# Seven load buffers instead of ten, and the casts of later head pairs tied to the scores three pairs back

## The chip, the cores and the metric

The kernel runs on one core of a Trainium2 chip. The metric is the device time of one execution in microseconds, as the median over executions. The profile is one execution taken by the hardware profiler; its span is a little shorter than the device time. Names in the profile: PE is TensorE's matmuls, PEld its weight loads, DVE is VectorE, ACT ScalarE, POOL GpSimd, SP SyncE; SPq and POOLq are their DMA queues. L491 is line 491 of the kernel; lines differ by a few between versions. An execution counts as slow when it takes over 1.5% longer than the fastest of the same kernel, and as fast otherwise; only fast ones are compared. The granted clock is the share of its full speed that TensorE was given.

## The reference, cut to what matters

```python
# attention: batch 4, 8 heads, 768 tokens, head size 64
scores = q @ k.T / 8;  masked by blocks of 32;  attn = softmax(scores);  x = attn @ v
# then a mixing block on x (4, 768, 512)
u  = x + lam * (w_tok @ (alpha1 * x + beta1))
out = u + lam * (relu((alpha2 * u + beta2) @ w_ch1) @ w_ch2)
```

The kernel handles the heads in 16 pairs, numbered 0 to 15, and runs attention of later pairs beside the mixing of earlier batches.

## The kernel before

The kernel is written as a list of jobs with priorities. A list scheduler in the kernel's own code decides, at build time, in which order each engine's instructions stand; on the chip each engine runs its own list strictly in that order and waits with semaphores. So a change of one dependency can move many instructions, and an instruction that waits holds up everything behind it on its engine.

From pair 6 on, q and k reach TensorE in four steps: a load by GpSimd's queue into a buffer "ld"; a cast by VectorE into a staging tile "rel"; two DMA transposes by SyncE's queue into qx and kx; the score matmuls. V takes only a load and a cast.

```python
slots = dict(sps=2, mm=2, cp=1, ops=1, eT=NET, head=NQB, vext=NV, ld=10, rel=2, ...)

ld[p, nm] = load(nm, pair_ap(src, *pairs[p]), [P, 2, NT * D], dt, "ld", 10, ...)   # 192 KB each

# pairs 6 to 15
rels[p] = wk.tile([P, 2, NT, P], BF, name="rel", tag="rel", bufs=2)
cq = cast_job(p, 0, "q2", stage_of(p, 0), (3, p, 0), ("rel",))        # VectorE
ck = cast_job(p, 1, "k2", stage_of(p, 1), (3, p, 1), (), [cq])        # VectorE
def xt(p=p):                                                          # SyncE
    for i, dst in enumerate((qx, kx)):
        nc.sync.dma_start_transpose(dst[slot_of(p)]..., rels[p][:, i, :, :]...)
# ... cut: scores, exp on ScalarE, mask minimum on VectorE, attn @ v, mixing
```

An eviction, below, is the instruction that takes a finished matmul result out of TensorE's result buffer; the ReLU eviction writes the tile "hts". A mask minimum (tile "eT") applies the mask to a piece of the attention weights.

There are two staging tiles. The q cast of pair p writes the tile that pair p-2 used, so it waits until both transposes of pair p-2 have landed.

The softmax here doesn't subtract the row's maximum and nothing guards it: scores larger than these inputs give would overflow.

Of the kernel before, what the change touches and what calls it, by code (L numbers as in the profile page):

```python
# [21 lines left out]
D = 64  # L22
# [5 lines left out]
P = 128  # L28
NT = S // P
# [6 lines left out]
NU = 9  # L36
NS = NPAIR * NU
NPE = 6
NET = 11
LEAD = 18  # L40
AHEAD = 13000.0
SCALE = 1.0 / 8.0
EXPB = -0.35667494
# [21 lines left out]
def kernel(  # L65
# [47 lines left out]
    NQB = 4  # L113
    NV = 3
# [6 lines left out]
    vext = [  # L121
        pp.tile([P, 2, NT, VW], F16, name=f"vext{i}", tag=f"vext{i}") for i in range(NV)
    ]
# [18 lines left out]
    def pair_ap(src, b, n):  # L142
        return src[b, 2 * n : 2 * n + 2].rearrange("h (p o) d -> p h (o d)", o=NT)
# [54 lines left out]
    def first_cast(a):  # L198
        for i, src in enumerate((q2f, k2f)):
            sl = src[:, a, :].rearrange("p (o d) -> p o d", o=NT)  # L200
            dst = rel0[:, a, :, i * D : (i + 1) * D]
            if a == 0 and i == 1:
                nc.scalar.copy(out=dst, in_=sl)
            else:
                nc.vector.tensor_copy(out=dst, in_=sl)
# [25 lines left out]
    for j in range(2, NQB):  # L231
# [11 lines left out]
    DRAIN = 166.0  # L243
    free_at = dict(NONE=0.0, PE=T0, ACT=T0, DVE=T0, POOL=4800.0, SP=T0)
    slots = dict(
        sps=2, mm=2, cp=1, ops=1, eT=NET, head=NQB, vext=NV, ld=10, rel=2,
        x=NXB, uT=3, hts=2, a1p=2, ub=2, ot=2, w2b=1,
    )
    jobs = []
# [35 lines left out]
    def mmt(n, cols):  # L285
        return n * (max(cols, 60) / 2.4 + 2.7)

    def dve(n, rate, base):
        return base + n / 0.96 / rate

    pairs = [(b, n) for b in range(B) for n in range(NPAIR)]
# [4 lines left out]
    def Load(xfer, prio, fn, deps=(), take=()):  # L296
        j = Job("POOL", 720.0, prio, fn, deps, take)
        j.xfer = xfer
        return j

    def load(name, src_ap, shape, dt, tag, bufs, xfer, prio, deps=(), take=()):
        def fn():
            t = wk.tile(shape, dt, name=name, tag=tag, bufs=bufs)
            nc.gpsimd.dma_start(t[:], src_ap)
            return t

        return Load(xfer, prio, fn, deps, take)

    ld = {}
# [4 lines left out]
    def load_pair(p, prio, which="qkv"):  # L314
        for src, dt, nm in ((q, BF, "q2"), (k, BF, "k2"), (v, F16, "v2")):
            if p == 0 and nm != "v2" or nm[0] not in which:
                continue
            ld[p, nm] = load(
                nm, pair_ap(src, *pairs[p]), [P, 2, NT * D], dt, "ld", 10,
                1300.0 if p < 2 else 980.0, prio, take=("ld",),  # L320
            )

# [72 lines left out]
    for t in range(NT):  # L395
# [9 lines left out]
        j = Job("PE", mmt(NT, P), (5, t), tr, [wload["tok", t // 2]], take=("mm",))  # L405
# [25 lines left out]
    for g in range(4):  # L431
# [16 lines left out]
        j = Job("PE", mmt(16, 64), (5, 20 + g), bmm, [j_be2] + [wload["w1", i] for i in range(4)], take=("mm",))  # L448
# [34 lines left out]
    j = Job("DVE", 400.0, (3, 3, 9), mrow, [wtok_jobs[-1]])  # L483
    j = Load(5000.0, mout_prio, mout, [j])
# [4 lines left out]
    def cast_job(p, i, nm, dst_of, prio, take, deps=()):  # L489
        def fn():  # L490
            nc.vector.tensor_copy(  # L491
                out=dst_of(), in_=tl_ld(p, nm).rearrange("p h (o d) -> p h o d", o=NT)
            )

        return Job("DVE", dve(768, 4, 155), prio, fn, [ld[p, nm]] + list(deps), take=take, give=("ld",))

    def tl_ld(p, nm):
        return ld[p, nm].out[:]

    head_ready = {}  # L500

    def slot_of(p):
        return (2 * NPE + p - NPE) % NQB

    rels = {0: rel0}
    for p in range(len(pairs)):
        if p == 0:

            def fc():
                first_cast(1)  # L510

            def f_tr():
                tl["h0"] = transposes(rel0, 1)

            def f_cq(eng):
                copy(eng, qx[1][0:D, :], tl["h0"][0:D, :])

            def f_ck(eng):
                copy(eng, kx[1][0:D, :], tl.pop("h0")[D:P, :])

            head_ready[0] = Job("DVE", 1.0, (0, 0), lambda: None, take=("head", "rel"))
            j = Job("DVE", 720.0, (2, 0), fc)
            j = Job("PE", mmt(NT, P), (2, 0), f_tr, [j], take=("mm",))
            j = Copy((1, 0, 1), f_cq, [j, head_ready[0]], take=("head",))
            j = Copy((1, 0, 2), f_ck, [j], give=("mm", "rel"))

            def f_mb():
                nc.vector.tensor_copy(out=qx[1][MB, :], in_=qx[0][MB, :])

            jb = Job("DVE", 350.0, (2, 0, 1), f_mb)  # L530
            head_ready[1] = Job("NONE", 0.0, (0,), lambda: None, [j, jb], lat=0.0)
        elif p < NPE:

            def rel_of(p, i):
                def f():
                    if i == 0:
                        rels[p] = wk.tile([P, 2, NT, 2 * D], BF, name="rel", tag="rel", bufs=2)
                    return rels[p][:, :, :, i * D : (i + 1) * D]

                return f  # L540

            cq = cast_job(p, 0, "q2", rel_of(p, 0), (2, p, 0), ("rel",))
            ck = cast_job(p, 1, "k2", rel_of(p, 1), (2, p, 1), (), [cq])
            prev = head_ready[2 * p - 1]
            for a in range(2):
                h = 2 * p + a

                def tr(p=p, a=a, h=h):
                    tl["hd", h] = transposes(rels[p], a)

                def cpq(eng, h=h):
                    copy(eng, qx[h % NQB][0:D, :], tl["hd", h][0:D, :])

                def cpk(eng, h=h):
                    copy(eng, kx[h % NQB][0:D, :], tl["hd", h][D:P, :])

                jt = Job("PE", mmt(NT, P), (2, p, a), tr, [ck, prev], take=("mm", "head"),
                         give=("rel",) if a else ())
                j1 = Copy((1, p, a), cpq, [jt])
                j2 = Copy((1, p, a), cpk, [jt])  # L560
                prev = head_ready[h] = Job("NONE", 0.0, (0,), lambda: None, [j1, j2], give=("mm",), lat=0.0)
        else:

            def stage_of(p, i):
                def f():
                    if i == 0:
                        rels[p] = wk.tile([P, 2, NT, P], BF, name="rel", tag="rel", bufs=2)
                    return rels[p][:, i, :, :].rearrange("p o (h d) -> p h o d", h=2)

                return f  # L570

            cq = cast_job(p, 0, "q2", stage_of(p, 0), (3, p, 0), ("rel",))
            ck = cast_job(p, 1, "k2", stage_of(p, 1), (3, p, 1), (), [cq])

            def xt(p=p):
                for i, dst in enumerate((qx, kx)):
                    nc.sync.dma_start_transpose(
                        dst[slot_of(p)][:].rearrange("p (o c) -> p o c", o=NT),
                        rels[p][:, i, :, :].rearrange("p o c -> p (o c)"),
                    )  # L580

            prev = [head_ready[2 * NPE - 1]] if p == NPE else [head_ready[2 * p - 2]]
            jx = Job("SP", 2600.0, (1, p), xt, [ck] + prev, take=("head",), lat=2500.0,
                     give=("rel",))
            jx.slow = True
            head_ready[2 * p] = head_ready[2 * p + 1] = jx
# [4 lines left out]
    qk_jobs, exp_jobs = {}, {}  # L591
    eTs, ops = {}, {}
# [199 lines left out]
    for p in range(len(pairs)):  # L792
        b, n = pairs[p]

        def pv_put(p=p):
            nc.vector.tensor_copy(
                out=vext[p % NV][:, :, :, 0:D],
                in_=tl_ld(p, "v2").rearrange("p h (o d) -> p h o d", o=NT),
            )

        putv[p] = Job("DVE", dve(768, 4, 155), (2 if p == 0 else 3, p, 2), pv_put, [ld[p, "v2"]],
                      take=("vext",), give=("ld",))
        if p >= NPE:
            paired(p)
        else:
            single(p)


    uTs = {}
    ut_jobs = {}  # L810
    for p in range(len(pairs)):
# [67 lines left out]
        if b == 0:  # L879
# [9 lines left out]
            j = Job("PE", mmt(NT, P), (2, p, 9), utr, ubs, take=("mm",), give=("ub",))  # L889
# [16 lines left out]
    for kk in range(2 * B):  # L906
        b, hf = divmod(kk, 2)
        relus = []
        for f in range(16):
# [18 lines left out]
            def rl(eng, kk=kk, f=f):  # L928
# [5 lines left out]
                else:  # L934
# [11 lines left out]
            j = Job("PE", mmt(4, HS), (5, kk, f), c1, deps, take=take,  # L946
                    give=("uT",) if hf == 1 and f == 15 else ())
# [82 lines left out]
    def gated(j):  # L1030
        return j.gate is not None and j.gate >= NS and j.gate - NS > st["ch"] / rate + LEAD

# [20 lines left out]
    while left:  # L1053
        moved = True
        while moved:
            moved = False
            for e in free_at:
                if free_at[e] > t:
                    continue
                best = None  # L1060
                if e == "POOL" and dma_free[0] - t > AHEAD:
                    seq += 1
                    heapq.heappush(events, (dma_free[0] - AHEAD, -seq, None))
                    continue
# [10 lines left out]
                j = best[1]  # L1075
# [45 lines left out]
        while events and events[0][0] <= t:  # L1121
            _, _, j = heapq.heappop(events)
# [45 lines left out]
```

## Time and profile before

| | before |
|---|---|
| median of the first group of runs | 325.51 us (324.99 to 326.92) |
| span of the profiled run | 324.5 us |
| PE busy | 305.8 us, 94% |
| DVE, ACT busy | 206.8, 208.1 us, 64% each |

TensorE is the limit, but not all the time. The windows view gives the busy microseconds of each engine in a stretch (the count of its instructions in brackets). These lines are of the kernel before.

```profile
70.00:80.00 10.00, 9.95 (x135) 7.04 (x133) 8.94 (x21) 7.77 (x9) 5.33 (x8) 1.00 1.46 180
80.00:90.00 10.00, 7.91 (x85) 5.04 (x85) 6.90 (x13) 6.41 (x9) 1.65 (x3) 1.00 1.36 161
90.00:100.00 10.00, 6.29 (x51) 3.12 (x51) 5.37 (x12) 5.29 (x7) 1.39 (x2) 1.00 1.42 139
100.00:110.00 10.00, 9.89 (x108) 5.22 (x109) 9.22 (x19) 5.76 (x8) 2.80 (x4) 1.00 1.04 155
```

The first number after the stretch's length is PE; then come PEld, DVE, ACT, POOL, the granted clock, and two figures of the DMA engines. From 80 to 100 us TensorE is busy 14.20 of 20 us, so it loses 5.80 us there. TensorE's weight loads and VectorE too are less busy in that stretch than on either side of it, so neither is short of time there: something makes them wait. The waits view of the kernel before names it (who waited for whom: us in total, times, longest).

```profile
DVE rel L491 <- DMA kx<-rel: 7.7, 2, 4.6
PE mm L920 <- DVE hts L935: 3.7, 2, 3.5
PE mm L920 <- DVE x_sb L857: 1.9, 1, 1.9
```

VectorE stood twice, 7.7 us together, at a q cast that waited for a kx transpose. TensorE in turn waited for VectorE. VectorE's timeline of the kernel before (start, duration, instruction, in brackets the idle time before it and what ended it) shows what stood behind the two casts.

```profile
87.09 0.36 DVE L491 COPY rel<-q 128x768 bf16<-128x768 bf16 x1 [3.10 <-DMA kx<-rel]
...
92.69 0.36 DVE L491 COPY rel<-k 128x768 bf16<-128x768 bf16 x1
93.01 0.69 DVE L747 TENSOR_TENSOR eT<-eT,maskT 128x1024 f16<-128x1024 f16 x1
98.34 0.36 DVE L491 COPY rel<-q 128x768 bf16<-128x768 bf16 x1 [4.63 <-DMA kx<-rel]
98.61 0.61 DVE L935 TENSOR_SCALAR hts<-mm,b1t 128x384 bf16<-128x384 f32 x1
99.14 0.68 DVE L747 TENSOR_TENSOR eT<-eT,maskT 128x1024 f16<-128x1024 f16 x1
...
107.31 0.35 DVE L796 COPY vext<-v 128x768 f16<-128x768 f16 x1
```

The cast at 87.09 is pair 9's, the one at 98.34 pair 10's. Behind the second stands the ReLU eviction of 98.61, whose input was complete by about 94.5 us. The last line, pair 9's v cast, is a landmark. TensorE waited for that eviction, by its own timeline:

```profile
95.20 0.60 PE L716 MATMUL sps<-qx,kx 64*128 64x512 bf16 x4
99.28 0.81 PE L920 MATMUL mm<-uT,w1b 128*128 128x384 bf16 x4 [3.47 <-DVE hts L935]
```

### The profile page before, as it was taken

The page shows a single profiled execution, that of the slowest core. Times are in us where ns is not written, and L with a number is a line of the kernel's source. Part 1 is how long each engine was busy: PE and PEld are TensorE (multiplying, and loading weights), DVE is VectorE, ACT ScalarE, POOL GpSimd, SP SyncE. Part 2 cuts the span into 40 slices and gives each one's busy share as a digit, 9 for nine tenths or more (in the row PEclk, how much of TensorE's full clock was granted, in tenths as well). Part 3 has the DMA queues.
Part 4 walks back from the last instruction along what each step waited for, and adds up shares of the span by engine and source line. Part 5 has one row for each costly group of instructions (what it writes and reads, how often), then busy time and mean ns, then how long its engine had stood idle before and what let it go on. Part 6 is the DMA issues. An engine that isn't in the chain of part 4 may idle for free.

```text
span 324.5 us, 7574 instructions
## 1 busy us (share of the span) xinstructions
PE 305.8 (94%) x3209; PEld 189.3 (58%) x3238; DVE 206.8 (64%) x406; ACT 208.1 (64%) x264; POOL 44.2 (14%) x69
## 2 busy tenths in 40 slices
PE   7889989899777999999999999999999999999996
PEld 3566868667434556654655655655655565455544
DVE  4559876778657987786969687776878660201001
ACT  4999998897664567866666667755783625354530
POOL 4747312425102201000000000000000000000000
PEclk9999989999999999999999999999999999999999
DMA  5999999999999974304042231003010201201102
GB/s 138 193 247 210 208 242 164 250 189 166 161 123 171 165 138 73 52 34 105 34 43 64 59 85 24 2 34 89 3 26 34 57 34 24 94 5 40 59 19 79
DMA packets 46774, 31.95 MB, mean 98 GB/s; under 512 B 27516, under 2 KB 42264, under 8 KB 46612
## 3 DMA queue, kind: packets, MB, share of 16 engines
q0 software_dynamic: 16496, 17.83, 32.9%
q1 hardware_dynamic: 29992, 13.40, 20.6%
q8 instruction: 25, 0.41, 0.5%
q10 hardware_dynamic: 252, 0.24, 0.3%
q14 instruction: 9, 0.07, 0.1%
HBM read 32.04 MB, written 7.47 MB: 122 GB/s over the span
## 4 chain that ended last, share of the span: by engine, by line
PE 78%; DMA 10%; ACT 7%; DVE 3%; issue 1%; POOL 0%; DVEq 0%; ACTq 0%
PE mm L920 22%; PE cp L965 21%; PE mm L847 8%; PE ops L774 8%; PE sps L716 7%; ACT eT L653 6%; DMA w2b<-in_moe_w_ch_dram 6%; DMA kx<-rel 4%; PE ops L965 4%; PE sps L638 2%; PE sps L920 2%; PE cp L168 1%; ACT kx L268 1%; PE ops L678 1%; DVE hts L935 1%
## 5 line engine op out<-in xcount | busy, mean ns | idle before, releaser
L742 ACT ACTIVATE eT<-sps 128x1024 f16<-128x1024 f32 x90 | 88.3, 1020 | 29.9 <-PE sps L716 28.7
L920 PE MATMUL mm<-uT,w1b 128*128 128x384 bf16 x472 | 90.6, 326 | 5.9 <-DVE hts L935 3.7
L931 ACT ACTIVATE hts<-mm,b1t 128x384 bf16<-128x384 f32 x91 | 52.9, 581 | 62.0 <-PE mm L920 59.4
L965 PE MATMUL cp<-w2b,hts 128*128 128x512 bf16 (+1 forms) x308 | 75.7, 374 | 1.5
L747 DVE TENSOR_TENSOR eT<-eT,maskT 128x1024 f16<-128x1024 f16 x90 | 61.2, 687 | 15.5 <-ACT eT L742 15.4
L920 PEld LDWEIGHTS <-w1b 128*128 128x128 bf16 x512 | 47.1, 97 | 40.2 <-issue 10.1
L653 ACT ACTIVATE eT<-sps 128x1024 f16<-128x1024 f32 (+1 forms) x55 | 52.9, 1016 | 5.8 <-PE sps L638 5.1
L965 PEld LDWEIGHTS <-hts 128*128 128x128 bf16 x400 | 36.4, 98 | 33.6 <-issue 0.8
L982 DVE TENSOR_TENSOR ot<-x_sb,cp 128x512 f32<-128x512 f32 (+1 forms) x21 | 14.1, 673 | 45.9 <-PE cp L965 45.5
L774 PEld LDWEIGHTS <-eT 128*128 128x128 f16 x720 | 29.9, 97 | 16.1 <-issue 3.8
L847 PE MATMUL mm<-a1p,wtokT 128*128 128x128 bf16 x576 | 37.0, 220 | 0.1
L638 PE MATMUL sps<-qx,kx 88*128 88x512 bf16 (+1 forms) x144 | 32.0, 331 | 5.3 <-ACT eT L653 4.2
L774 PE MATMUL ops<-vext,eT 128*128 128x65 f16 x720 | 35.8, 194 | 0.0
L847 PEld LDWEIGHTS <-wtokT 128*128 128x128 bf16 x576 | 33.1, 98 | 2.0 <-issue 1.0
L716 PE MATMUL sps<-qx,kx 64*128 64x512 bf16 (+1 forms) x240 | 27.3, 327 | 0.0
L857 DVE TENSOR_TENSOR x_sb<-x_sb,mm 128x384 f32<-128x384 f32 x32 | 17.7, 552 | 9.4 <-PE mm L847 9.2
L678 PEld LDWEIGHTS <-eT 128*128 128x128 f16 x432 | 19.6, 99 | 6.0 <-issue 0.9
L935 DVE TENSOR_SCALAR hts<-mm,b1t 128x384 bf16<-128x384 f32 x27 | 16.6, 616 | 7.4 <-PE mm L920 7.3
L638 PEld LDWEIGHTS <-kx 88*128 88x128 bf16 x144 | 12.8, 98 | 11.3 <-issue 6.9
L716 PEld LDWEIGHTS <-kx 64*128 64x128 bf16 x240 | 8.2, 94 | 15.7 <-issue 12.7
L863 DVE TENSOR_TENSOR ub<-x_sb,a_bc 128x384 bf16<-128x384 f32 x32 | 17.1, 554 | 0.2
L613 DVE TENSOR_TENSOR x_sb<-ops,rcp 128x384 f32<-128x384 f32 x28 | 15.6, 558 | 1.0
(74 smaller groups left out, 221.7 us busy)
## 6 DMA issues: line engine op xcount, KB each, us to landing
out_dram<-ot SPq DMA_DIRECT2D x23, 256.0 KB, 2.0
v<-in_v_dram POOLq DMA_DIRECT2D x16, 192.0 KB, 9.1
q<-in_q_dram POOLq DMA_DIRECT2D x15, 192.0 KB, 10.9
k<-in_k_dram POOLq DMA_DIRECT2D x15, 192.0 KB, 9.9
w1b<-in_moe_w_ch_dram POOLq DMA_DIRECT2D x4, 512.0 KB, 10.2
w2b<-in_moe_w_ch_dram POOLq DMA_DIRECT2D x4, 512.0 KB, 15.2
wtk<-in_moe_w_tok_dram POOLq DMA_DIRECT2D x3, 384.0 KB, 10.0
mask_rows<-maskT POOLq DMA_DIRECT2D x1, 1152.0 KB, 14.3
```

The costliest lines, as they stand in the source:

```text
L638: nc.tensor.matmul(sps[:, f - u * UN : f - u * UN + w], kx[h][0:KC, ts(jt, P)], qx[h][0:KC, c : c + w], start=True, stop=True,)
L653: nc.scalar.activation(eT[:, c], sps[:, c], AF.Exp, bias=EXPB, scale=SCALE)
L678: nc.tensor.matmul(ops[p, a][:, t * VW : t * VW + D + 1], eTs[p, u][:, ts(i - u * GU, P)], vx[:, a, jt, 0 : D + 1], start=(i % HT == 0), s ...
L716: nc.tensor.matmul(sps[:, a * 512 + lo : a * 512 + lo + w], kx[sl][r, ts(jt, P)], qx[sl][r, c : c + w], start=True, stop=True,)
L742: nc.scalar.activation(eT[:], sps[:], AF.Exp, bias=EXPB, scale=SCALE)
L747: nc.vector.tensor_tensor(out=e, in0=e, in1=maskT[:, u, :].unsqueeze(1).broadcast_to([P, 2, 512]), op=ALU.min,)
L774: nc.tensor.matmul(ops[p, a][:, t * VW : t * VW + D + 1], eTs[p, u][:, a * 512 + c * P : a * 512 + (c + 1) * P], vx[:, a, jt, 0 : D + 1], ...
L847: nc.tensor.matmul(tp[:, j, :], wtokT[:, s, ts(3 * g + j, P)], tl["a1p", p][:, s, :], start=(s == 0), stop=(s == NT - 1),)
L920: nc.tensor.matmul(hp[:, 0:HS], w1b[:, dk, ts(f, P)], uTs[b][:, dk, ts(hf, HS)], start=(dk == 0), stop=(dk == 3),)
L931: nc.scalar.activation(hts[kk][:, f, :], hp[:, 0:HS], AF.Relu, bias=b1t[:, f : f + 1], scale=1.0)
L935: nc.vector.tensor_scalar(out=hts[kk][:, f, :], in0=hp[:, 0:HS], scalar1=b1t[:, f : f + 1], scalar2=0.0, op0=ALU.add, op1=ALU.max,)
L965: nc.tensor.matmul(cps[kk, mi][:, 0:w], hts[kk][:, nk, ts(m, P)], w2tile[0][:, nk, lo : lo + w], start=(nk == 0), stop=(nk == 15),)
```

## The change

Its intent is a shorter prefetch: fewer buffers held by loads, and casts made nearer to their use.

```diff
+NLD = 7
-        ... vext=NV, ld=10, rel=2,
+        ... vext=NV, ld=NLD, rel=2,
-                nm, pair_ap(src, *pairs[p]), [P, 2, NT * D], dt, "ld", 10,
+                nm, pair_ap(src, *pairs[p]), [P, 2, NT * D], dt, "ld", NLD,
+    after = []
...
             cq = cast_job(p, 0, "q2", stage_of(p, 0), (3, p, 0), ("rel",))
+            if p > NPE + 1:                       # pairs 8 to 15
+                after.append((cq, (p - 3) * NU))  # unit 0 of the pair three back
...
+    for j, i in after:
+        j.deps.append(qk_jobs[i])
```

No instruction is added or removed. What moves is decided by the scheduler: on VectorE the pair-10 q cast now stands two places later, behind the eviction and the minimum shown above, and the casts of pairs 11 to 15 stand later by 7 to 20 mask minimums (of 9 per pair). TensorE's and ScalarE's orders change mainly in the second half of the kernel.

More of the change, by code (lines that the diff above doesn't have):

```diff
@@ L245 @@
     slots = dict(
-        sps=2, mm=2, cp=1, ops=1, eT=NET, head=NQB, vext=NV, ld=10, rel=2,
+        sps=2, mm=2, cp=1, ops=1, eT=NET, head=NQB, vext=NV, ld=NLD, rel=2,
         x=NXB, uT=3, hts=2, a1p=2, ub=2, ot=2, w2b=1,
```

## The prediction

> **What bounds the kernel now.** TensorE. The page gives it 305.8 of 324.5 us, and the windows view shows 99% busy from 100 to 280 us. It loses about 8 us in the first 80 us, 3.3 in the tail, and 2.1 + 3.7 = 5.8 in the windows 80-90 and 90-100 (busy 7.91 and 6.29 of 10). Only that last part is near what the change touches.
>
> **Why it idles there.** The waits view has "DVE rel L491 <- DMA kx<-rel: 7.7, 2, 4.6". VectorE runs in order, and twice it stands at the q cast of a pair, because the staging tile has two buffers and the transpose two pairs back has not landed: 84.0 to 87.1 us (pair 9) and 93.7 to 98.3 us (pair 10), by its timeline. Behind the second stand a ReLU eviction (98.61) and a mask minimum (99.14); TensorE's matmul at 99.28 waits 3.47 us for that eviction. The chain of waits holds the same transpose: issued at 85.44, 12.78 us, where kx<-rel usually takes 2.8 (list of DMA issues). It coincides with loads: sixteen q/k/v loads are issued from 56 to 81 us and land about every 1.3 us until 93. The Trainium skill, "DMA: Bandwidth & Descriptors", section "Issuing engines are not separate DMA queues", says that DMAs of all issuing engines share 16 engines and interleave; the trace agrees (both queues carry packets in the same microseconds).
>
> **What the change does.** The work is identical: same instructions per engine; GpSimd's order is unchanged, the others' nearly so up to 100 us. Comparing orders:
> 1. The pair-10 q cast moves behind that eviction and minimum, so the 4.6 us stall no longer holds them.
> 2. The casts of pairs 11 to 15 move later (pair 11 from mask unit 11 to 18, pair 15 from 40 to 54-60). A pair takes about 17.6 us, so they still lead their scores by 40 us or more: no starvation.
> 3. With seven buffers a load waits for the cast seven back, not ten. By the cast times of the trace, loads up to q11 keep their times within about 3 us (k6 and v6 slip behind a queue that is full anyway; mask and second-layer weights do not move). k11, v11 and q12, issued at 78 to 81 us before, must wait for the pair-9 and pair-10 casts (87 us on). Some 0.6 MB less is then queued against the pair-8 transpose, which should land earlier than 98.2.
>
> **On the critical path.** The first stall stays: order and load queue are the same until 87 us. Of the second, if the transpose landed no earlier, TensorE would still meet a shortened wait a group or two later, about 2 us saved (estimate from the timeline's durations); if it lands by 95 us, nearly all 3.5 is saved. I take 2.9. After that TensorE is saturated, so the shift survives to the end; the reordering after 190 us should move it under 0.5.
>
> **Predicted:** 322.4 us, range 320.2 to 325.2; faster by over 2% 0.05, within 2% 0.94, slower 0.01.
>
> **What would show it.** Waits: the 7.7 us VectorE wait on kx<-rel falls to 3-4, the 3.5 us TensorE wait on hts to under 1.5. Windows: 90-100 rises to over 8.5 busy, 80-90 stays near 7.9, 100-280 stays 99%. GpSimd timeline: k11 issued after 85 us. Pair-8 kx lands in under 10 us.
>
> **What would make it wrong.** The pair-8 transpose being slow for another reason than loads (at 92-98 us few load packets move); a new VectorE stall at a later cast; the k6/v6 delay reaching the mask; the first gap vanishing too, which gives up to 5.8 us.

## The result

Four runs of the changed kernel took 321.58 to 321.90 us, median 321.75, against 325.51 us of the kernel before. The ratio is 0.9878 (95% interval 0.9845 to 0.991). Ratios in this document are the mean time of one kernel's fast runs over that of the other's in the same rounds, so they are not quite the ratios of the medians quoted. Two further groups gave 0.9868 and 0.9888.

The windows of the changed kernel:

```profile
70.00:80.00 10.00, 9.98 (x129) 6.57 (x128) 8.49 (x20) 7.51 (x9) 4.18 (x6) 1.00 1.48 142
80.00:90.00 10.00, 7.07 (x78) 4.53 (x78) 6.38 (x12) 4.82 (x6) 0.70 (x1) 1.00 1.40 142
90.00:100.00 10.00, 10.00 (x90) 5.04 (x89) 8.17 (x17) 7.49 (x11) 2.10 (x3) 1.00 1.25 156
100.00:110.00 10.00, 10.00 (x126) 5.92 (x123) 8.41 (x15) 5.94 (x7) 0.70 (x1) 1.00 0.65 128
```

The stretch from 90 to 100 us is now full; the one from 80 to 90 is not. The waits view of the changed kernel:

```profile
DVE rel L492 <- DMA kx<-rel: 4.5, 2, 3.6
PE mm L927 <- DVE x_sb L864: 2.6, 1, 2.6
PE mm L927 <- DVE hts L942: 0.2, 1, 0.2
```

VectorE's timeline of the changed kernel, the lines that answer to those above:

```profile
86.13 0.36 DVE L492 COPY rel<-q 128x768 bf16<-128x768 bf16 x1 [3.62 <-DMA kx<-rel]
...
93.57 0.62 DVE L942 TENSOR_SCALAR hts<-mm,b1t 128x384 bf16<-128x384 f32 x1 [0.83 <-PE mm L927]
94.11 0.68 DVE L751 TENSOR_TENSOR eT<-eT,maskT 128x1024 f16<-128x1024 f16 x1
95.68 0.36 DVE L492 COPY rel<-q 128x768 bf16<-128x768 bf16 x1 [0.90 <-DMA kx<-rel]
...
103.02 0.35 DVE L800 COPY vext<-v 128x768 f16<-128x768 f16 x1
```

The eviction and the minimum run first, at 93.57 and 94.11; then VectorE still waits for the transpose, but only 0.90 us, and TensorE has work meanwhile. The first stall is no shorter. The matmuls on TensorE that answer to those above follow each other without a wait:

```profile
94.24 0.61 PE L720 MATMUL sps<-qx,kx 64*128 64x512 bf16 x4
94.78 0.82 PE L927 MATMUL mm<-uT,w1b 128*128 128x384 bf16 x4
```

Three landmarks place the gain. The pair-9 q cast comes 87.09 - 86.13 = 0.96 us earlier, the pair-9 v cast 107.31 - 103.02 = 4.29 us earlier, the end of the span 324.5 - 320.1 = 4.4 us earlier. So 3.3 us were won between the two casts, at the second stall, and about 0.1 us in all the 213 us after it.

The 0.96 us at the first landmark was won before the second stall, and it is not shown to be the change's. With the instructions of the two profiles set side by side, the changed kernel gains 1.62 us between 46 and 52 us. There TensorE's granted clock stood at half from 46.5 to 49.9 us in the profile of before; the profile of the changed kernel lists no such stretch, but a second profile of the same changed kernel, after_again, has one (46.9 to 50.4 us) and gains nothing there. It is 0.48 us ahead just before the first stall. So the gain of 4.4 us between this pair of profiles holds some 1.6 us of luck, partly offset by a slower start and a longer first stall.

From 60 to 80 us TensorE was idle 0.76 us in the profile of before and 0.13 in that of the changed kernel. Over all profiles taken here in the fast state it was 0.6 to 1.7 us in the six with ten load buffers (before and five experiments) and at most 0.2 in five of the seven with seven or eight, but 0.98 (loads_only) and 2.40 (behind2) in the other two. So fewer buffers may be worth half a microsecond there; the spread is too large to say.

### The profile page after: what moved, and what is told of

The parts are those of the page before. It is cut to its first block, busy times and chain, and to the rows that moved or that the text cites. A ratio compares the mean times of both kernels' runs of the same rounds, so it can differ in the third digit from the quotient of the medians.

```text
span 320.1 us, 7610 instructions
## 1 busy us (share of the span) xinstructions
PE 306.0 (96%) x3238; PEld 187.7 (59%) x3238; DVE 206.9 (65%) x406; ACT 207.8 (65%) x264; POOL 44.4 (14%) x69
## 4 chain that ended last, share of the span: by engine, by line
PE 78%; ACT 7%; DMA 7%; DVE 4%; POOL 1%; issue 1%; DVEq 0%; ACTq 0%
PE mm L927 23%; PE cp L972 22%; PE mm L854 8%; PE ops L778 8%; PE sps L720 7%; ACT eT L657 5%; PE ops L972 4%; DMA kx<-rel 4%; PE sps L642 3%; DMA k<-in_k_dram 2%; PE sps L927 2%; ACT kx L269 2%; PE ops L682 1%; DVE x_sb L864 1%; DMA q2f<-in_q_dram 1%
## 5 line engine op out<-in xcount | busy, mean ns | idle before, releaser
L746 ACT ACTIVATE eT<-sps 128x1024 f16<-128x1024 f32 x90 | 88.3, 1020 | 31.3 <-PE sps L720 30.1
L972 PE MATMUL cp<-w2b,hts 128*128 128x512 bf16 (+1 forms) x336 | 80.3, 374 | 0.0
L927 PEld LDWEIGHTS <-w1b 128*128 128x128 bf16 x512 | 46.9, 97 | 37.2 <-issue 7.6
L642 PE MATMUL sps<-qx,kx 88*128 88x512 bf16 (+1 forms) x144 | 31.2, 324 | 5.1 <-ACT eT L657 4.0
```

Source lines behind the costliest of these rows:

```text
L642: nc.tensor.matmul(sps[:, f - u * UN : f - u * UN + w], kx[h][0:KC, ts(jt, P)], qx[h][0:KC, c : c + w], start=True, stop=True,)
L746: nc.scalar.activation(eT[:], sps[:], AF.Exp, bias=EXPB, scale=SCALE)
L927: nc.tensor.matmul(hp[:, 0:HS], w1b[:, dk, ts(f, P)], uTs[b][:, dk, ts(hf, HS)], start=(dk == 0), stop=(dk == 3),)
L972: nc.tensor.matmul(cps[kk, mi][:, 0:w], hts[kk][:, nk, ts(m, P)], w2tile[0][:, nk, lo : lo + w], start=(nk == 0), stop=(nk == 15),)
```

## The experiments

Theory A: TensorE's loss from 80 to 100 us comes from VectorE standing at the two q casts, and the change shortens the second stand by both its halves, the new place of the cast and the lighter queue of loads. Rival B: later casts of pairs 11 to 15 relieve VectorE. Rival C: only the lighter load queue counts. Rival D: the transposes are slow by themselves, not because of loads.

Twelve runs (repeats and two controls of the changed kernel among them) were made in three groups, each on another chip and with five rounds against the kernel before. These groups were noisier than the first: the kernel before took 324.3 to 328.8, 323.8 to 328.3 and 323.6 to 328.0 us in them (two more executions of the second group, 330.07 and 331.14 us, are slow), so a single ratio is known to about 0.4 to 0.6%. Edits are shown shortened, against the changed kernel unless said otherwise.

### The two halves apart: loads_only and casts_only, each twice

```diff
 loads_only:                              casts_only:
 NLD = 7                                 -NLD = 7
-if p > NPE + 1: after.append(...)       +NLD = 10
                                          (casts as in the changed kernel)
```

The built orders make this a clean cross: loads_only has the order of before on every engine, and casts_only that of the changed kernel on every engine; only the loads' waits for buffers differ.

> Seven load buffers, casts where they were before. The order on every engine is that of the kernel before; only the waits of the loads differ. Theory A (the second VectorE stall, at the pair-10 q cast, is what the change shortens, by both of its halves): k11, v11, q12 wait for the pair-9 casts, the pair-8 kx transpose lands some 2 to 3 us earlier after its issue, the stall of 4.6 us falls to about 2, time about 2 us below before (323.5). Rival B (the gain is the later casts of pairs 11 to 15, which relieve VectorE): time as before. Rival C (only the lighter load queue counts): time as the changed kernel, 3.8 us below before.

> Ten load buffers, casts behind the scores three pairs back. The order on every engine is that of the changed kernel; only the waits of the loads differ. Theory A: the pair-8 kx transpose lands as late as before (about 12 to 13 us after issue), VectorE still stalls 2 to 3 us at the pair-10 q cast, but the eviction and the minimum are already done, TensorE loses 1 to 2 us there instead of 3.5; time about 2 us below before. Rival B: 3.8 us below before, as the changed kernel. Rival C: as before.

> The run loads_only once more, because its ratio (0.9955, interval 0.9909 to 1.0001) left open whether the smaller number of load buffers is worth anything by itself, and its profile spoke against my reason: the second VectorE stall was 5.4 us, not shorter. If the lighter queue is worth about 2 us as predicted: ratio near 0.994 and a second stall under 3 us in this profile. If it is worth nothing alone: ratio 0.997 to 1.003 and a second stall of 4 to 6 us again.

> The run casts_only once more, beside loads_only_2 and the changed kernel on one chip. If the order of the casts carries the change: ratio 0.988 to 0.992, within 0.3% of the changed kernel. If the two halves share it: about 0.994.

> The changed kernel as the control of this group: ratio 0.986 to 0.990.

| | ratio to before (interval) | TensorE idle, 80 to 100 us | VectorE's wait at the pair-10 q cast |
|---|---|---|---|
| before | 1 | 5.80 us | 4.63 us |
| loads_only | 0.9955 (0.9909 to 1.0001) | 5.78 us | 5.43 us |
| loads_only_2 | 0.9978 (0.9938 to 1.0019) | 4.06 us | 2.20 us |
| casts_only | 0.9924 (0.9881 to 0.9967) | 3.32 us | 2.05 us |
| casts_only_2 | 0.9969 (0.9918 to 1.0019) | 2.23 us | 1.01 us |
| changed kernel | 0.9878 (0.9845 to 0.991) | 2.93 us | 0.90 us |
| after_3, the same | 0.9888 (0.9843 to 0.9932) | profile in the slow state | not read |

The idle column is 20 us less the PE sum of the two windows 80-90 and 90-100. The profile of after_3 (351.89 us, clock 0.851) is not used.

The order alone cuts TensorE's idle time in that stretch by 2.5 to 3.6 us in both profiles. The smaller number of buffers alone cut it by nothing in one profile and by 1.7 us in the other, and neither of its two timed ratios is clear of 1. Rival C falls: in one group loads_only_2 gave 0.9978 (from 0.9938 on) and the changed kernel 0.9888 (up to 0.9932). Not all expectations were met: loads_only's stall was to fall to about 2 us and was 5.43; loads_only_2 showed the ratio that was expected if the loads are worth nothing and the short stall that was expected if they are worth something; casts_only_2, at 0.9969, missed both values named for it.

A second measure from the traces is less noisy than the times: the stretch from the start of the ReLU eviction at 81.31 us, ahead of both stalls, to pair 9's v cast behind them. It took 26.00 us before, 23.19 and 22.09 us in the changed kernel (after_again is the second), 23.81 and 22.79 us in casts_only and its repeat, 23.58 us in two_places below. So over both stalls the order alone won 2.2 to 3.2 us, and the whole change 2.8 to 3.9. The two loads_only profiles took 28.54 and 25.40 us, but in them TensorE's granted clock stood at half for 6.8 us (96.1 to 103.0) and 3.4 us (88.3 to 91.7), right after TensorE had idled 2.8 and 2.1 of the 3.4 us before. So a stall can be followed by slow matmuls, which its idle time does not count, and what fewer buffers alone are worth at this place stays open. In the kernel before TensorE idled up to 3.3 of 3.4 us and was not slowed in this stretch, so this does not follow every stall.

The mean of the two groups is 0.997 for loads alone and 0.995 for casts alone; multiplied that is about 0.991, where the changed kernel gave 0.988. With these intervals it is open whether the two halves help each other or whether this is noise.

### Only two places: two_places

```diff
-if p > NPE + 1:
-    after.append((cq, (p - 3) * NU))
+if p > 9:
+    after.append(cq)
...
-for j, i in after:
-    j.deps.append(qk_jobs[i])
+for j in after:
+    j.deps.append(min_jobs[6 * NU + 7])
```

With ten buffers. The built order equals that of before on TensorE, ScalarE, GpSimd and SyncE; on VectorE the pair-10 q cast stands two places later and the pair-11 one a place earlier, nothing else. (Binding pair 10 alone does not do this: built that way, but not run, the scheduler lets pair 11 take the staging tile first, and VectorE's places stay as they were.)

> Ten load buffers, and of the new order of casts only this: the pair-10 q cast stands behind the ReLU eviction and the mask minimum that it preceded (and the pair-11 q cast one place earlier, behind it). TensorE, ScalarE, GpSimd and SyncE orders are those of before. Theory A: the whole worth of the new cast order is here, so the time is that of casts_only within 0.6 us, about 2 us below before. Rival B (later casts of pairs 11 to 15): no gain, as before within 0.5 us.

Measured: ratio 0.9894 (0.9852 to 0.9937), TensorE idle from 80 to 100 us 2.72 us (its windows 8.43 and 8.85 busy). With the casts of pairs 12 to 15 where they were, and TensorE's order untouched, it gets at least what the whole new order got with ten buffers (0.9924 and 0.9969). Rival B expected no gain and falls as the main cause. In two_places VectorE still waits 1.4 us at the cast, but the eviction stands ahead of it.

### Without the loads: noload, which missed its aim, and noload_all

```diff
 def fn():
+    if skip: return None                   # shortened; noload: pairs 9 to 12; noload_all: 9 to 15
     t = wk.tile(shape, dt, name=name, tag=tag, bufs=bufs)
     nc.gpsimd.dma_start(t[:], src_ap)
...
 def tl_ld(p, nm):
+    if skipped(p): return wtokT[:, 0:2, 0 : NT * D]
     return ld[p, nm].out[:]
```

Both kernels are made from the kernel before (ten buffers, no cast moved). They have its orders, less the loads, and give a wrong result (relative errors 0.53 and 0.71).

> The kernel before with its orders, but pairs 9 to 12 load no q, k, v: their casts read the token weights that lie in SBUF (a wrong result on purpose). It tests why the transposes land late. If the loads slow them (theory A): with no load in flight from about 77 us, the pair-7 and pair-8 kx transposes land within some 5 us of issue instead of 12 to 13, both VectorE stalls (3.1 and 4.6 us) go, and the time falls by 5 to 6 us below before, past the changed kernel. If the transposes are slow by themselves or by their own queue (rival D): both stalls stay and the time moves less than 1 us.

Measured: 0.986 (0.9811 to 0.9908). The first stall stayed (3.45 us) and the second went. It was a poor test: GpSimd, in want of nothing, went on at once to the loads of pairs 13 to 15, and loads landed every 1.3 us until 90.8 us, as before.

> As noload, but no pair from 9 on loads anything (wrong result on purpose). The run without the loads of pairs 9 to 12 did not test what it was for: GpSimd went straight on to the loads of pairs 13 to 15, so loads still landed every 1.3 us until 90.8 and the first stall stayed (3.45 us). Here the last load lands near 78 us. Loads slow the transposes: the packets of transposes, of which about 190 a microsecond start while loads alternate with them, start at over 400 a microsecond from 78 us on; the pair-7 kx transpose lands by about 81 us, both stalls (3.1 and 4.6 us) go; time 5 to 6 us below before. Rival D (transposes slow by themselves): first stall stays at about 3 us, time no more than 4 us below before.

Measured: 0.9818 (0.9772 to 0.9864), median 320.56 against 326.07 us of the fast executions before, 5.5 us less. Its windows:

```profile
80.00:90.00 10.00, 9.93 (x100) 5.95 (x100) 9.38 (x17) 7.41 (x11) 0.00 (x0) 1.00 0.41 59
90.00:100.00 10.00, 9.89 (x104) 5.48 (x103) 8.29 (x19) 7.68 (x10) 0.00 (x0) 1.00 0.57 108
```

No wait on kx<-rel is left in its waits view. The trace's DMA packets show how loads slow a transpose. Counted by the microsecond in which they start, load packets / transpose packets:

```
us        71       72       ...   79       ...   86       87       88       89       90       91
before    200/196  188/193        121/96         200/202  195/192  195/195  181/291  126/319  42/415
noload_all 197/195 192/195        0/917          0/0      0/0      0/0      0/0      0/0      0/0
```

While both queues have work, they start about the same number of packets, 195 and 195 in a microsecond. A load packet is about 720 bytes on average there and a transpose packet 256. One transpose of 192 KB is 800 packets, so it takes some 4 us behind loads (an estimate: 800 / 195), and the transposes queue behind one another on top. Without loads up to 917 transpose packets started in one microsecond, and by the packet count the pair-7 kx transpose, issued at 75.6 us, was through at about 80.1; in the kernel before it was issued at 75.3 and through at about 86.3, just before the first stall ended. The Trainium skill, "DMA: Bandwidth & Descriptors", section "Queues, rings and completion order", says that each DMA engine goes round-robin between queues packet by packet; the equal counts agree with it. (The page's packet usually holds several descriptors. Whether a packet of the profile is one of these, and the single turns, the trace does not tell.) Rival D falls as the main reason: without the loads the stalls are gone.

One part stays unexplained. In the kernel before, from 92 to 96 us, few packets of either queue start and each takes longer (load packets 104 to 163 ns on average, transpose packets 28 to 108, where 74 and 31 were usual just before). That tail held up the pair-8 kx transpose too, and no run took it apart. The packets also show stops of nearly the whole DMA: from 83.4 to 84.5 us and from 97.2 to 97.8, both during VectorE's waits, at most 6 packets of the two queues start in a tenth of a microsecond, against 110 just after the second. noload_all has such stops (81.2 to 81.8 and 92.8 to 93.3 us) with no load in flight. So the loads do not cause these, and a part of rival D stands: transposes are at times held up by something that no run here names.

### Remove the wait itself: rel3 and rel3_old_order

```diff
-    rels[p] = wk.tile([P, 2, NT, P], BF, name="rel", tag="rel", bufs=2)
+    rels[p] = wk.tile([P, 2, NT, P], BF, name="rel", tag="rel", bufs=3)    # at every "rel" tile
```

A staging tile takes 3 KB per partition, as much as two load buffers; with ten load buffers it does not fit (such a build is refused: 114.06 KB asked, 111.06 left). rel3 is the changed kernel with this (seven load buffers, the scheduler's rel=3 as well); its order is that of the changed kernel on every engine. rel3_old_order is the kernel before with this and eight load buffers, no cast moved; its order is that of before but for one exchange of neighbours on VectorE.

> The changed kernel with three staging tiles for the casts instead of two (the room of the three load buffers given up is enough for one). Order on every engine is that of the changed kernel. The pair-9 q cast no longer waits for the pair-7 kx transpose, and the pair-10 one waits for a transpose that landed 5 us earlier. Theory A (VectorE's stalls at the casts are what stops TensorE at 80 to 100 us): both stalls go, TensorE's windows 80-90 and 90-100 are both above 9.5 of 10, time 2 to 3.5 us below the changed kernel (318.5 to 320). If TensorE's loss in 80-90 has another cause, the time stays that of the changed kernel.

> The kernel before with its own order on every engine (but for one exchange of neighbours on VectorE), with a third staging tile paid for by two load buffers (eight instead of ten). No cast is moved. Theory A: both stalls go without any reordering, TensorE's windows 80-90 and 90-100 are above 9.5, ratio 0.979 to 0.985, as rel3. If the late casts of pairs 11 to 15 were worth something of their own (rival B), it stays 1 us or more behind what rel3 reached (0.981).

> The changed kernel again, as the control of this group: 3 to 4.5 us below before (ratio 0.986 to 0.991).

The windows of rel3:

```profile
80.00:90.00 10.00, 9.89 (x106) 6.09 (x107) 9.38 (x18) 7.48 (x11) 0.78 (x2) 1.00 1.12 142
90.00:100.00 10.00, 9.95 (x105) 5.34 (x107) 7.76 (x16) 7.07 (x10) 2.10 (x3) 1.00 1.19 165
```

Its VectorE timeline shows the same two casts with no wait before them:

```profile
83.06 0.35 DVE L492 COPY rel<-q 128x768 bf16<-128x768 bf16 x1
...
92.34 0.35 DVE L492 COPY rel<-q 128x768 bf16<-128x768 bf16 x1
```

| | ratio to before (interval) | median, us | TensorE idle, 80 to 100 us |
|---|---|---|---|
| after_again (the changed kernel) | 0.9868 (0.9816 to 0.992) | 322.34 | 1.66 us |
| rel3 | 0.9811 (0.9754 to 0.9867) | 319.98 | 0.16 us |
| rel3_old_order | 0.9863 (0.9807 to 0.992) | 320.60 (five fast executions) | 0.00 us |

With a third staging tile both stalls are gone, in either order (rel3_old_order keeps one wait of 0.4 us on kx<-rel, which TensorE does not feel). rel3 was 2.4 us faster than the changed kernel in the same group by the medians; the two intervals overlap, so the size is not firm. rel3_old_order was in another group; its five fast executions spread from 319.8 to 323.6 us (a sixth, 325.31, is slow), and the expected range of 0.979 to 0.985 was just missed. Its profile is of one of the quickest (319.83 us) and shows a full TensorE from 80 to 110 us; of the others there is no profile.

The traces say more than the times here. The stretch from the eviction to pair 9's v cast, 26.00 us before, is 20.00 us in both, and 19.99 in noload_all. So the stalls go without moving any cast, and 6.0 us is what they cost. What the late casts, with the reordering that comes with them, are worth by themselves (what is left of rival B) shows behind that v cast. From there to the end of the span the five profiles with the new order (the changed kernel, after_again, casts_only and its repeat, rel3) gain 0.13 to 0.15 us on the kernel before, and the four with the old one (loads_only and its repeat, two_places, rel3_old_order) at most 0.01.

### Casts two pairs back: behind2

```diff
-    after.append((cq, (p - 3) * NU))
+    after.append((cq, (p - 2) * NU))
```

> The changed kernel with the casts placed behind the scores two pairs back instead of three: the pair-9 q cast moves from mask unit 3 to 8, the pair-10 one from 8 to 19. Theory A: the first stall has nothing left to wait for by then, so it goes as well, and the time falls 2 to 3 us below the changed kernel, if the casts are still early enough (they lead their scores by over 25 us). If casts that late starve the scores, it is slower than the changed kernel and the waits view shows scores waiting on qx<-rel.

Measured: 0.9816 (0.9769 to 0.9864), median 319.90 us. The pair-9 q cast now runs at 95.6 us without a wait, TensorE is busy 9.91 and 9.88 of 10 us in the two windows, and no score waits for qx<-rel. So with the first cast moved out of the loads' way as well, the stalls are gone just as with a third tile. The built order moves more than casts: two ReLU evictions go from VectorE to ScalarE, and what they are worth is not told apart. rel3 and behind2 are the fastest correct kernels here and equal within noise; they beat the kernel before by about 1.9% and the changed kernel by about 2 us.

## Why the prediction was right, and where it was not

The time was predicted as 322.4 us (320.2 to 325.2) and measured as 321.75. In the prediction's words:

- **What bounds it, and where the loss is: right.** 3.3 of the 4.4 us of span won lie at the second stall; the kernel after it kept its pace. The 0.96 us before it goes with a half-clock stretch that the profile of before had and that of the changed kernel does not list.
- **Step 1, the two places on VectorE: right, and it is the larger part of the change.** two_places alone gave 0.9894, the whole order with ten buffers 0.9924 and 0.9969, the changed kernel 0.9868 to 0.9888; over both stalls the order won 2.2 to 3.2 us of the 2.8 to 3.9. TensorE's wait for hts fell from 3.5 to 0.2 us (predicted under 1.5).
- **Step 2, no starvation by the later casts: right.** From the pair-9 v cast to the end the two kernels differ by about 0.1 us.
- **Step 3, the lighter load queue: its mechanics right, its worth overstated.** k11 was issued at 86.8 us (predicted after 85), and noload_all shows that loads do slow the transposes. But "pair-8 kx lands in under 10 us" failed: it was issued at 84.19 us and released the cast at 95.68, 11.5 us later, where it had been 12.9. (That is close to the 95 us named, but half of the gain over 98.34 is its earlier issue.) In loads_only the stall was no shorter at all, in its repeat it was 2.20 us. (The 2.8 us that the prediction calls usual is the figure of the list of DMA issues; the trace tells the landing of one of the ten kx transposes only.) The loads queued before the stall had landed by 90.8 us in the changed kernel and by 92.8 before, a small difference against the landing by 95 us instead of 98.2 that was hoped for, and the unexplained slow tail came after it.
- **The first stall stays: right.** 3.10 us before, 3.62 after; 1.7 us in after_again. The waits on kx<-rel came to 4.5 us, a little over the predicted 3 to 4.
- **The size.** 2.9 us were predicted for the second stall and 3.3 won there by the landmarks, nearly the 3.5 named as the most to be had. By the medians 3.1 us were predicted and 3.76 measured. The closeness is in part luck: 2.9 was a guess between 2 and 3.5, the quick landing that it leaned on did not come, and a second profile of the same kernel won 2.5 us at the second stall and 1.4 at the first. The gain came for the larger part because the eviction no longer stood behind the cast, so that TensorE had work during the shorter wait, and not because the transpose landed soon.

## What to carry to other kernels

On an engine that runs in order, look at what stands behind an instruction that waits for a DMA: putting two instructions that are soon ready ahead of it won 2.4 us here by the trace of two_places, and 3.2 us by its medians, while fewer load buffers alone won nothing that the times could tell from zero. A staging buffer more at the place where the wait is can be worth more than many prefetch buffers that feed the queue one waits for: trading two load buffers for one staging tile removed both stalls. Before two profiles are subtracted, look at the granted clock in each: a half-clock stretch of 3.4 us cost 1.6 us. And an experiment that removes some transfers from a queue must be checked for what moves up into their place.

## What the Trainium skill lacked or had wrong

- "DMA: Bandwidth & Descriptors", section "Queues, rings and completion order": the packet-wise round-robin is stated, and the equal counts agree with it (about 195 packets of each queue in a microsecond). What it lacks is the consequence for queues with unlike packets: transpose packets of 256 bytes shared evenly by count with load packets of about 720, so the transposes got about a quarter of the bytes and fell from up to 917 to 195 packets a microsecond.
- The same page, section "Issuing engines are not separate DMA queues", calls the sequencer's time to initiate a DMA usually small relative to the DMA itself. Here issuing one transpose held SyncE for 1.21 us at best, where a kx transpose took 2.79 us to land (the one of ten whose landing the trace of before tells), and for 4.26 us (5.94 in casts_only) behind a loaded queue, for a transpose that took 12.8.
- "Perfetto Trace Analysis", section "Identifying Performance Opportunities" (under "Optimization Strategy"), says that consistent bubbles, the same gap repeating, can mean too little room in SBUF or PSUM for the next tile. Here two waits of VectorE, of 3.10 and 4.63 us, were enough to make two gaps on TensorE, and a third staging tile removed both (rel3). The page does not say that the engine that shows the bubble, TensorE, may be two steps away from the buffer that is short.
- No page has the slow tail, 104 to 163 ns per load packet from 92 to 96 us against 74 before it, or the stops of 0.5 to 1.1 us in which nearly no packet of either queue starts, with loads in flight (before) and without (noload_all); their cause is open.
